# A hand-written issue order for two batches of attention and a feed-forward layer: the third batch's maxima moved

## The chip, the cores and the metric

One core of a Trainium2 chip runs the whole program. The metric is device time in microseconds (us) of one execution, the median of several runs. A core has five engines that each work through their own list of instructions in order: TensorE (PE; its weight loads are listed apart as PEld), VectorE (DVE), ScalarE (ACT), GpSimd (POOL) and SyncE (SP), which here issues all transfers. An instruction waits on semaphores for what it needs, and all that stands behind it on its engine waits with it.

## The reference

For each of 8 batches and 8 heads (576 tokens, head size 64), K and V are first condensed into 32 memories by softmax weights, then every query attends to these memories. The heads side by side are the input of a feed-forward layer (512 to 2048 to 512):

```python
a = np.exp(phi - np.max(phi, axis=2, keepdims=True))        # phi: batch, head, 576 tokens, 32 memories
a = a / (np.sum(a, axis=2, keepdims=True) + 1e-09)          # softmax over the tokens
k_m = np.einsum('bhsm,bhsd->bhmd', a, k)
v_m = np.einsum('bhsm,bhsd->bhmd', a, v)
scores = np.matmul(q, k_m.transpose(0, 1, 3, 2)) / np.sqrt(64)
attn = softmax(scores)                                      # over the 32 memories
x = np.matmul(attn, v_m)                                    # heads side by side: 4608 tokens x 512
h = x @ w_in
out = (h * np.clip(h + 3.0, 0.0, 6.0) / 6.0) @ w_out
```

All is float32 at the interface. The kernel splits operands of its matmuls into a high part (TensorE's rounded float32) and a low part, and adds three products.

## The kernel before

The product of memories V and `w_in` is taken once per batch ("fold"), so that the first layer of the feed-forward part multiplies it with the attention weights themselves. The work behind that is cut into **slots**: slot n is one tile of 128 hidden columns for one part of a batch's tokens (256 tokens, or 320, of which 64 are kept for a later slot of two batches together). Slots 0 to 71 belong to the first two batches. A slot's steps are named by a letter and its number:

- `g.n`: first matmul (L409, PE, 6 matmuls into a PSUM tile `ph`, of which there are two); `u.n`: relu (L419, ACT, into `gf`, of which there are two); `m.n`: gate (L423, DVE, reads `ph` and `gf`); `k.n`: the gate of the 64 tokens kept (L428, DVE); `h.n`, `l.n`: high and low part of the result (L437 on ACT, L441 on DVE); `a.n`: second matmul (L452, PE, 6 matmuls), which runs three slots later.

The attention part of batch b has steps of its own: `pt.b`, `pn.b` load phi transposed and in natural layout (L201), `kv.b.t` loads five tiles of K and V (L207), `q.b.half` loads queries (L213); `mx.b` takes the maxima over tokens (L236, DVE). These stand one per partition and are needed along a row: for the first two batches TensorE turns them (`md`, `me`), from the third on they go out to DRAM (`mo.b`, L241, a transfer of single values) and come back to all partitions (`sp.b`, L246, into `nmxb`). Then `xa.b.part` subtracts them (L261, DVE), `xe` is the exponential (L265, ACT), `kvm.b.t` the matmuls over tokens (L273, PE), `sc` scores (L311), `cs`, `dm`, `bl` softmax steps (L342, L354, L367, on GpSimd but for the first half of the first batch), `fo.b.c` the fold (L376, PE) and `vh`, `vl` its high and low part (L387, L392).

The weights arrive as 64-bit words and are turned into float32 by six steps on ACT and DVE (`ab`, `ro`, `cl`, `sh`, `si`, `to`); `sx.u`, `sy.u` split `w_out` (L179 on ACT, L183 on GpSimd), `wk.c` stores a finished quarter of `w_in` to DRAM (L174). `recall` (L503) reads back partial outputs, which `e0`, `e1` (L479) add to the result of a slot's last matmul, and `fetch` (L191) reads back `w_in`.

The order is written out by hand: `BEGIN` is a list of such words, and `play` issues them one by one. Each engine's list is the words that concern it, in that order:

```python
    def play(words):
        for word in words:
            name, *args = word.split(".")
            n = [int(x) for x in args]
            if name in WEIGHTS:
                WEIGHTS[name](*n)
            elif name in SLOT:
                SLOT[name](slots[n[0]])
```

From slot 72 on another table orders the batches 2 to 7; it is not touched.

Of the kernel before, what the change touches and what calls it, by code (L numbers as in the profile page):

```python
# [50 lines left out]
q.0.0 xa.0.0 xa.0.1 xe.0.0 raw2.0 xa.0.2 xe.0.1 cl.0.0.0 xe.0.2 sh.0.0.0 q.0.1 ab.0.0.1 si.0.0.0 ro.0.0.1
raw2.1 kvm.0.0 cl.0.0.1 kvm.0.1 sh.0.0.1 si.0.0.1 kvm.0.2 to.0.0.0 kvm.0.3 kvm.0.4 nr.0 to.0.0.1 nk.0 tp.0 tk.0
sc.0.0 ab.1.0 pt.1 ct.0.0 pn.1 kv.1.0 kv.1.1 kv.1.2 kv.1.3 ro.1.0 cm.0.0 kv.1.4 sc.0.1 cs.0.0 warm.4 cl.1.0
ex.0.0 ds.0.0 wk.0 ab.1.1 dr.0.0 dm.0.0 ro.1.1 q.1.0 mx.1 fo.0.0 bt.0.0 raw2.2 md.1 bh.0.0 ct.0.1 me.1 vh.0.0.0
q.1.1 warm.3 vh.0.0.1 cm.0.1 xa.1.0 raw2.3 cs.0.1 vl.0.0.0 xe.1.0 vl.0.0.1 ex.0.1 xa.1.1 kvm.1.0 sh.1.0 xe.1.1
kvm.1.1 raw.1.0 xa.1.2 si.1.0 xe.1.2 kvm.1.2 raw.1.1 kvm.1.3 raw.1.2 ds.0.1 kvm.1.4 to.1.0 raw.1.3 raw2.4
cl.1.1 sx.0 nr.1 dr.0.1 nk.1 sh.1.1 dm.0.1 bl.0.0 tp.1 raw2.5 ro.1.2 sy.0 si.1.1 tk.1 g.0 sc.1.0 u.0 g.1 bt.0.1
u.1 to.1.1 bh.0.1 ro.1.3 bl.0.1 ct.1.0 sx.1 m.0 fo.1.0 cm.1.0 h.0 ab.0.1.0 m.1 cs.1.0 g.2 l.0 g.3 h.1 sy.1
cl.0.1.0 ex.1.0 a.0 u.2 ds.1.0 vh.1.0.0 vh.1.0.1 m.2 l.1 h.2 g.4 dr.1.0 u.3 vl.1.0.0 dm.1.0 a.1 ab.0.1.1
vl.1.0.1 m.3 sc.1.1 l.2 h.3 bt.1.0 u.4 g.5 l.3 bh.1.0 ct.1.1 a.2 bl.1.0 u.5 m.4 k.4 h.4 cm.1.1 ro.0.1.0 g.6 m.5  # L60
cs.1.1 k.5 l.4 a.3 h.5 l.5 ex.1.1 sh.0.1.0 g.7 u.6 ds.1.1 e0.3 a.4 m.6 u.7 k.6 dr.1.1 h.6 m.7 g.8 dm.1.1 k.7
h.7 l.6 a.5 l.7 u.8 bt.1.1 ro.0.1.1 g.9 m.8 si.0.1.0 bh.1.1 a.6 u.9 bl.1.1 h.8 e1.3 g.10 ro.1.4 m.9 eo.3 a.7
cl.0.1.1 h.9 ro.1.5 l.8 to.0.1.0 g.11 u.10 a.8 e0.7 sh.0.1.1 ab.1.2 m.10 si.0.1.1 g.12 h.10 l.9 to.0.1.1 u.11
a.9 m.11 l.10 h.11 g.13 cl.1.2 u.12 ab.1.3 l.11 a.10 m.12 k.12 sh.1.2 u.13 g.14 e1.7 h.12 si.1.2 eo.7 fo.1.1
raw.2.0 raw.2.1 raw2.6 raw2.7 raw.2.2 raw.2.3 wk.1 m.13 a.11 k.13 h.13 l.12 to.1.2 vh.1.1.0 u.14 g.15 vh.1.1.1
raw.3.0 a.12 vl.1.1.0 sx.2 m.14 k.14 h.14 l.13 sy.2 g.16 l.14 u.15 a.13 m.15 u.16 k.15 cl.1.3 h.15 g.17
ab.0.2.0 m.16 a.14 l.15 sh.1.3 u.17 h.16 si.1.3 g.18 ro.0.2.0 a.15 m.17 k.17 h.17 l.16 to.1.3 u.18 g.19 ro.1.6
a.16 ro.0.2.1 vl.1.1.1 m.18 sx.3 l.17 g.20 cl.0.2.0 a.17 u.19 sy.3 sh.0.2.0 h.18 ro.1.7 fo.0.1 m.19 k.19 h.19
l.18 g.21 l.19 u.20 m.20 vh.0.1.0 a.18 si.0.2.0 u.21 h.20 ab.0.2.1 g.22 m.21 k.21 l.20 a.19 vl.0.1.0 u.22 h.21
to.0.2.0 vh.0.1.1 g.23 a.20 m.22 raw.3.1 raw.3.2 l.21 h.22 g.24 cl.0.2.1 u.23 a.21 ab.1.4 l.22 m.23 k.23  # L70
sh.0.2.1 u.24 g.25 h.23 si.0.2.1 ro.0.3.0 a.22 m.24 l.23 h.24 cl.1.4 g.26 u.25 e0.22 to.0.2.1 a.23 e0.23 m.25
raw.3.3 k.25 h.25 e1.22 g.27 ab.0.3.0 sh.1.4 eo.22 l.24 si.1.4 u.26 a.24 vl.0.1.1 ro.0.3.1 m.26 e1.23 g.28 h.26
l.25 eo.23 wk.2 to.1.4 u.27 a.25 fo.0.2 m.27 sx.4 k.27 l.26 g.29 cl.0.3.0 u.28 sy.4 a.26 h.27 sh.0.3.0 vh.0.2.0
vh.0.2.1 m.28 l.27 h.28 g.30 si.0.3.0 u.29 a.27 ab.0.3.1 m.29 k.29 l.28 h.29 g.31 to.0.3.0 u.30 a.28 vl.0.2.0
ab.1.5 m.30 l.29 g.32 h.30 cl.0.3.1 u.31 a.29 l.30 m.31 u.32 k.31 cl.1.5 h.31 g.33 m.32 sh.0.3.1 h.32 a.30 l.31
sh.1.5 u.33 si.0.3.1 g.34 a.31 si.1.5 m.33 k.33 h.33 l.32 g.35 to.0.3.1 u.34 a.32 to.1.5 wk.3 ab.1.6 pt.2 pn.2
kv.2.0 kv.2.1 kv.2.2 kv.2.3 kv.2.4 vl.0.2.1 sx.5 m.34 l.33 h.34 g.36 sy.5 u.35 l.34 a.33 m.35 q.2.0 u.36 k.35
cl.1.6 h.35 g.37 ab.1.7 m.36 a.34 l.35 sh.1.6 u.37 h.36 si.1.6 g.38 fo.0.3 m.37 k.37 h.37 l.36 a.35 to.1.6 u.38
vh.0.3.0 vh.0.3.1 g.39 a.36 vl.0.3.0 sx.6 m.38 l.37 h.38 sy.6 g.40 u.39 l.38 a.37 m.39 u.40 k.39 cl.1.7 h.39
# [5 lines left out]
nr.2 m.49 nk.2 k.49 h.49 tp.2 e0.46 g.50 tk.2 e1.46 sc.2.0 u.50 l.49 eo.46 a.47 m.50 ct.2.0 h.50 cm.2.0 g.51
e0.47 cs.2.0 sc.2.1 e1.47 u.51 a.48 l.50 ex.2.0 eo.47 pn.3 kv.3.0 kv.3.1 kv.3.2 kv.3.3 ct.2.1 kv.3.4 pt.3 m.51
g.52 cm.2.1 h.51 a.49 u.52 k.51 cs.2.1 l.51 m.52 fetch.2.1 g.53 ds.2.0 h.52 ex.2.1 l.52 a.50 dr.2.0 u.53 ds.2.1
q.3.0 dm.2.0 m.53 g.54 k.53 h.53 dr.2.1 recall.1.0 bt.2.0 a.51 dm.2.1 u.54 l.53 bh.2.0 recall.1.1 m.54 g.55
bl.2.0 bt.2.1 h.54 a.52 l.54 u.55 bh.2.1 m.55 k.55 h.55 g.56 bl.2.1 l.55 fo.2.0 u.56 m.56 a.53 h.56 mx.3
vh.2.0.0 vh.2.0.1 g.57 vl.2.0.0 mo.3 vl.2.0.1 a.54 u.57 l.56 m.57 k.57 h.57 g.58 l.57 a.55 u.58 m.58 h.58 g.59  # L90
l.58 a.56 u.59 m.59 k.59 h.59 g.60 sp.3 q.3.1 fetch.2.2 l.59 a.57 u.60 m.60 h.60 g.61 l.60 a.58 u.61 m.61 k.61
h.61 g.62 l.61 a.59 u.62 m.62 h.62 g.63 l.62 a.60 u.63 m.63 k.63 h.63 a.61 h.64 l.63 l.64 a.62 h.65 l.65 a.63
e0.62 h.66 e1.62 a.64 l.66 eo.62 h.67 e0.63 e1.63 h.68 a.65 l.67 l.68 h.69 a.66 eo.63 l.69 h.70 a.67 l.70 h.71
a.68 l.71
# [604 lines left out]
```

## Time and profile before

| | |
|---|---|
| median of 3 runs | 751.16 us (749.7 to 752.16) |
| the profiled execution's own time | 751.13 us |
| its span, first to last instruction | 749.4 us |
| busy: PE, DVE, ACT, POOL | 94%, 60%, 48%, 10% |

The span is what the rows below divide up; 1.7 us of the execution lie around it. Shares of busy time are means over a start in which the weights are prepared and VectorE has most to do, and a long rest in which TensorE hardly stops.

### The profile page before, as it was taken

To read this page: it belongs to the slowest core of one execution; us is meant where nothing else is said; L and a number is where in the kernel's file an instruction comes from. 1 tells how busy PE (TensorE), PEld (TensorE's weight loads), DVE (VectorE), ACT (ScalarE), POOL (GpSimd) and SP (SyncE) were. 2 spreads that over 40 slices of the span, in tenths; PEclk is the share of its full clock that TensorE was granted. 3 is DMA by queue.
4 is the path that set the end of the run, shared out by engine and by line. 5 is a ranking of instruction groups with operands and counts; after the bars stand their busy time and mean duration, and the time that the engine had idled before them with its cause. 6 is when DMAs were issued, how large, how long until landed. Compare 5 with 4: busy or idle time off the path is not lost.

```text
span 749.4 us, 12233 instructions
## 1 busy us (share of the span) xinstructions
PE 707.3 (94%) x4706; PEld 565.7 (75%) x4706; DVE 446.5 (60%) x999; ACT 361.5 (48%) x765; POOL 78.5 (10%) x59
## 2 busy tenths in 40 slices
...
GB/s 329 373 417 42 225 169 141 251 28 155 311 177 58 132 218 13 143 64 329 8 148 57 68 281 8 148 58 288 48 133 78 72 57 57 57 113 1 1 1 70
DMA packets 26042, 99.77 MB, mean 133 GB/s; under 512 B 4224, under 2 KB 4992, under 8 KB 21376
## 3 DMA queue, kind: packets, MB, share of 16 engines
...
q8 instruction: 37, 0.61, 0.4%
...
## 4 chain that ended last, share of the span: by engine, by line
PE 70%; DVE 15%; DMA 7%; ACT 3%; issue 3%; SPq 1%; ACTq 0%; DVEq 0%
PE acc L452 42%; PE ph L409 20%; PE pv L376 3%; DMA raw<-in_w 2%; DVE glo L441 2%; PE pk L273 2%; DVE gf L423 2%; DVE tmp L161 2%; DMA kvt<-in_kv 2%; DMA ptile<-in_pt 1%; DVE pnat L261 1%; PE psc L311 1%; DVE tmp L153 1%; DMA nmx<-nmx 1%; DVE tmp L156 1%
## 5 line engine op out<-in xcount | busy, mean ns | idle before, releaser
L452 PE MATMUL acc<-w,ghi 128*128 128x512 f32 x1152 | 324.7, 400 | 0.5 <-DVE o L483 0.4
L452 PEld LDWEIGHTS acc<-w,ghi 128*128 128x128 f32 x1152 | 202.3, 189 | 59.6 <-issue 16.8
L419 ACT ACTIVATE gf<-ph,three 128x256 f32<-128x256 f32 (+1 forms) x256 | 127.9, 500 | 170.9 <-PE ph L409 158.3
L409 PEld LDWEIGHTS ph<-phi,both 128*128 128x128 f32 x1024 | 164.3, 190 | 46.4 <-DVE gf L423 10.2
L423 DVE SCALAR_TENSOR_TENSOR gf<-gf,ph 128x256 f32<-128x256 f32 x256 | 106.9, 418 | 152.1 <-ACT gf L419 150.9
L409 PE MATMUL ph<-phi,both 128*128 128x320 f32 (+1 forms) x1024 | 183.2, 301 | 13.6 <-DVE rest L428 6.9
L452 PE MATMUL acc<-w,glo 128*128 128x512 f32 x576 | 184.7, 396 | 0.0
L437 ACT CAST ghi<-gf 128x256 fp32r<-128x256 f32 x256 | 103.9, 406 | 125.3 <-DVE gf L423 124.9
L441 DVE TENSOR_TENSOR glo<-gf,ghi 128x256 fp32r<-128x256 f32 x256 | 121.7, 477 | 49.4 <-ACT ghi L437 49.3
L452 PEld LDWEIGHTS acc<-w,glo 128*128 128x128 f32 x576 | 108.4, 188 | 25.6 <-DVE glo L441 0.4
L409 PE MATMUL ph<-plo,both 128*128 128x256 f32 (+1 forms) x512 | 110.2, 297 | 0.7 <-DVE plo L367 0.7
L409 PEld LDWEIGHTS ph<-plo,both 128*128 128x128 f32 x512 | 83.0, 190 | 1.0 <-DVE plo L367 1.0
L392 DVE TENSOR_TENSOR both<-pv,both 128x512 fp32r<-128x512 f32 x64 | 43.7, 688 | 42.0 <-ACT both L387 41.9
L342 POOL TENSOR_TENSOR st<-st,mx 128x640 f32<-128x640 f32 (+1 forms) x15 | 18.5, 1231 | 385.3 <-DVE mx L338 382.9
L387 ACT CAST both<-pv 128x512 fp32r<-128x512 f32 x64 | 36.6, 583 | 1.7 <-PE pv L376 1.6
L376 PE MATMUL pv<-w,kvT 64*32 64x512 f32 x512 | 35.7, 615 | 0.3 <-DVE both L392 0.3
L273 PE MATMUL pk<-kvt,pnat 128*32 128x129 f32 (+1 forms) x640 | 24.2, 295 | 9.1 <-DMA kvt<-in_kv 8.8
L273 PEld LDWEIGHTS pk<-kvt,pnat 128*32 128x32 f32 (+1 forms) x640 | 17.5, 115 | 16.5 <-ACT tmp L145 6.4
L183 POOL TENSOR_TENSOR w<-tmp,w 128x1024 fp32r<-128x1024 f32 x8 | 20.0, 2506 | 73.8 <-ACT w L179 73.8
L428 DVE SCALAR_TENSOR_TENSOR rest<-gf,ph 128x64 f32<-128x64 f32 x128 | 27.2, 213 | 0.0
L367 POOL TENSOR_TENSOR plo<-pT,phi 128x640 fp32r<-128x640 f32 (+1 forms) x15 | 21.7, 1445 | 36.6 <-ACT phi L362 36.6
L354 POOL TENSOR_TENSOR st<-st,sm 128x640 f32<-128x640 f32 (+1 forms) x15 | 17.8, 1184 | 50.2 <-DVE sm L350 50.2
...
## 6 DMA issues: line engine op xcount, KB each, us to landing
...
```

The source lines that it names most:

```text
L273: nc.tensor.matmul(self.pk[j * M : (j + 1) * M, g, :KV], self.pnat[:rows, t, g * P + j * M : g * P + (j + 1) * M], kvt[:rows, g * NJ + j, ...
L367: self.aux[hf].tensor_tensor(plo, self.pT[hf], probs[self.b, hf][0].bitcast(F32), ALU.subtract)
L376: nc.tensor.matmul(self.pv[c][j * M : (j + 1) * M, g, :], self.kvT[rows, g, j * M : (j + 1) * M], chunk[rows, j, :].bitcast(F32), start=Tr ...
L387: nc.scalar.copy(both[:, 0], self.pv[c][:, :, VC * k : VC * (k + 1)])
L392: nc.vector.tensor_tensor(both[:, 1], src, both[:, 0].bitcast(F32), ALU.subtract)
L409: nc.tensor.matmul(self.ph, w[:, g, fs], x[:, g * n : (g + 1) * n], start=(i == 0), stop=(i == len(seq) - 1),)
L419: nc.scalar.activation(self.gf, self.ph, AF.Relu, bias=three)
L423: nc.vector.scalar_tensor_tensor(gf[:, :n], gf[:, :n], 6.0, ph[:, :n], ALU.min, ALU.mult)
L428: nc.vector.scalar_tensor_tensor(kept, gf[:, n:], 6.0, ph[:, n:], ALU.min, ALU.mult)
L437: nc.scalar.copy(self.ghi, self.gated())
L441: nc.vector.tensor_tensor(self.glo, self.gated(), self.ghi.bitcast(F32), ALU.subtract)
L452: nc.tensor.matmul(accs[self.b, self.hf][0 if one else k], (self.glo if i == 2 else self.ghi)[:, k * P : (k + 1) * P], w2lo if i == 1 else ...
```

## The change

`BEGIN` is written anew. It holds the same 814 words, so every instruction and transfer is still there once; only their order differs. Two lines of the diff as an example, of slots 41 to 45:

```diff
-g.41 m.40 l.39 a.38 h.40 sh.1.7 u.41 vl.0.3.1 g.42 si.1.7 a.39 m.41 k.41 h.41 l.40 g.43 to.1.7 u.42 a.40 fo.1.2
-mx.2 sx.7 sy.7 m.42 mo.2 l.41 g.44 vh.1.2.0 vh.1.2.1 a.41 vl.1.2.0 u.43 vl.1.2.1 h.42 m.43 fo.1.3 k.43 h.43
...
+sh.1.7 sy.6 u.41 k.41 g.42 mx.2 a.39 m.41 mo.2 wk.3 vl.0.3.1 h.41 g.43 l.40 l.41 u.42 a.40 si.1.7 u.43 m.42
+fo.1.2 to.1.7 h.42 g.44 a.41 vh.1.2.0 l.42 sx.7 m.43 k.43 vl.1.2.0 g.45 h.43 sy.7 vh.1.2.1 l.43 a.42 u.44
```

`pt.2` and `pn.2` move from slot 35 to slot 27; the five `kv.2` and `q.2.0` move from slot 35 to slot 45, behind `sp.2`; `wk.3` moves from slot 35 to slot 42. `fo.2.0` moves from slot 56 to slot 62. Most other words move by less than one slot; on TensorE the order of `g` and `a` stays, and folds change places with them.

On SyncE, the transfers around the third batch's loads. Before:

```order
L174 DMA w_kept_77<-w_1042 128x2048
L174 DMA w_kept_78<-w_1280 128x2048
L201 DMA ptile<-in_pt 128x1152
L201 DMA pnat<-in_pn 128x1280
L207 DMA kvt<-in_kv 128x1032 x4
L207 DMA kvt<-in_kv 64x1032
L213 DMA qh<-in_qt 128x1024
L241 DMA nmx_1616<-nmx 128x2x1
L246 DMA nmxb<-nmx_1616 128x256
L503 DMA o<-partial_0_686 128x1024
```

And after the change:

```order
L174 DMA w_kept_77<-w_1045 128x2048
L201 DMA ptile<-in_pt 128x1152
L201 DMA pnat<-in_pn 128x1280
L241 DMA nmx_1568<-nmx 128x2x1
L174 DMA w_kept_78<-w_1277 128x2048
L246 DMA nmxb<-nmx_1568 128x256
L207 DMA kvt<-in_kv 128x1032 x4
L207 DMA kvt<-in_kv 64x1032
L213 DMA qh<-in_qt 128x1024
L503 DMA o<-partial_0_689 128x1024
```

The loads of phi no longer stand behind the store of the last quarter of `w_in`, and K, V and the first queries now stand behind the broadcast of the maxima.

On VectorE, around the third batch's maxima (`nmx<-ptile`; `tmp<-raw_7` are `si.1.7` and `to.1.7`). Before:

```order
L423 SCALAR_TENSOR_TENSOR gf<-gf,ph 128x256
L428 SCALAR_TENSOR_TENSOR rest<-gf,ph 128x64
L441 TENSOR_TENSOR glo<-gf,ghi 128x256
L171 ISA tmp<-raw_7_807,tmp 128x2048
L236 TENSOR_REDUCE nmx<-ptile 128x2
L423 SCALAR_TENSOR_TENSOR gf<-gf,ph 128x256
L441 TENSOR_TENSOR glo<-gf,ghi 128x256
```

And after the change:

```order
L428 SCALAR_TENSOR_TENSOR rest<-gf,ph 128x64
L236 TENSOR_REDUCE nmx<-ptile 128x2
L423 SCALAR_TENSOR_TENSOR gf<-gf,ph 128x256
L392 TENSOR_TENSOR both<-pv,both 128x512
L441 TENSOR_TENSOR glo<-gf,ghi 128x256 x2
L161 SCALAR_TENSOR_TENSOR tmp<-raw_7_805,tmp 128x1024
L423 SCALAR_TENSOR_TENSOR gf<-gf,ph 128x256
L171 ISA tmp<-raw_7_805,tmp 128x2048
```

The maxima now stand ahead of `m.41`, `vl.0.3.1`, `l.40`, `si.1.7` and `to.1.7`, which they followed.

On VectorE, around the first subtraction of these maxima (`pnat<-pnat,nmxb`, `xa.2.0`). Before, with `m.43` to `xa.2.1`:

```order
L423 SCALAR_TENSOR_TENSOR gf<-gf,ph 128x256
L428 SCALAR_TENSOR_TENSOR rest<-gf,ph 128x64
L441 TENSOR_TENSOR glo<-gf,ghi 128x256 x2
L423 SCALAR_TENSOR_TENSOR gf<-gf,ph 128x256
L392 TENSOR_TENSOR both<-pv,both 128x512
L261 TENSOR_TENSOR pnat<-pnat,nmxb 128x512
L423 SCALAR_TENSOR_TENSOR gf<-gf,ph 128x256
L428 SCALAR_TENSOR_TENSOR rest<-gf,ph 128x64
L392 TENSOR_TENSOR both<-pv,both 128x512
L441 TENSOR_TENSOR glo<-gf,ghi 128x256
L261 TENSOR_TENSOR pnat<-pnat,nmxb 128x512
```

And after the change, with `vl.1.2.0` to `m.46`:

```order
L392 TENSOR_TENSOR both<-pv,both 128x512
L441 TENSOR_TENSOR glo<-gf,ghi 128x256
L392 TENSOR_TENSOR both<-pv,both 128x512
L423 SCALAR_TENSOR_TENSOR gf<-gf,ph 128x256
L428 SCALAR_TENSOR_TENSOR rest<-gf,ph 128x64
L423 SCALAR_TENSOR_TENSOR gf<-gf,ph 128x256
L441 TENSOR_TENSOR glo<-gf,ghi 128x256 x2
L261 TENSOR_TENSOR pnat<-pnat,nmxb 128x512
L392 TENSOR_TENSOR both<-pv,both 128x512 x2
L261 TENSOR_TENSOR pnat<-pnat,nmxb 128x512
L423 SCALAR_TENSOR_TENSOR gf<-gf,ph 128x256
```

`m.45`, `k.45`, `l.44` and `l.45` now stand ahead of the subtraction instead of behind it, and `vl.1.3.0`, which was ahead, is behind.

## Rows read from the trace of the kernel before

**Rows 1.** The page: busy time and share of the span of each engine.

```profile
PE 707.3 (94%) x4706; PEld 565.7 (75%) x4706; DVE 446.5 (60%) x999; ACT 361.5 (48%) x765; POOL 78.5 (10%) x59
```

**Rows 2.** Five stretches: length, busy time of each engine, granted clock, DMA share, GB/s.

```profile
40.00:57.00 17.00, 10.05 (x65) 6.15 (x66) 13.71 (x18) 9.58 (x19) 9.35 (x5) 0.70 0.99 407
57.00:158.00 101.00, 95.85 (x558) 76.98 (x559) 97.23 (x183) 69.27 (x133) 18.85 (x10) 1.00 0.43 157
158.00:168.02 10.02, 9.67 (x71) 6.13 (x69) 6.51 (x11) 4.83 (x11) 2.39 (x1) 1.00 0.01 0
168.02:173.39 5.37, 0.00 (x1) 0.03 (x1) 1.30 (x4) 0.58 (x2) 0.00 (x0) 0.80 0.85 218
173.39:178.00 4.61, 4.61 (x16) 3.58 (x20) 3.70 (x10) 2.81 (x8) 0.00 (x0) 0.50 0.89 372
```

**Rows 3.** Chain that ended last, from 157 us: start, duration, what.

```profile
157.10 1.26 DVE nmx L236
158.40 7.45 DMA nmx<-nmx
165.86 6.21 DMA nmxb<-nmx
```

**Rows 4.** VectorE in order of time: start, duration, instruction, idle time before.

```profile
153.36 0.68 DVE L392 TENSOR_TENSOR both<-pv,both 128x512 fp32r<-128x512 f32 x1
155.43 0.20 DVE L428 SCALAR_TENSOR_TENSOR rest<-gf,ph 128x64 f32<-128x64 f32 x1
157.03 1.34 DVE L236 TENSOR_REDUCE nmx<-ptile 128x2 f32<-128x1152 f32 x1
158.62 2.31 DVE L441 TENSOR_TENSOR glo<-gf,ghi 128x256 fp32r<-128x256 f32 x1
...
172.09 0.69 DVE L261 TENSOR_TENSOR pnat<-pnat,nmxb 128x512 f32<-128x512 f32 x1 [7.27 <-DMA nmxb<-nmx]
172.70 0.41 DVE L423 SCALAR_TENSOR_TENSOR gf<-gf,ph 128x256 f32<-128x256 f32 x1
```

**Rows 5.** TensorE in order of time, slots 43 and 47, with `a.40` and `a.44`.

```profile
156.21 0.76 PE L409 MATMUL ph<-phi,both 128*128 128x320 f32 x4
158.03 0.63 PE L452 MATMUL acc<-w,glo 128*128 128x512 f32 x2
...
173.39 1.41 PE L409 MATMUL ph<-phi,both 128*128 128x320 f32 x4 [5.37 <-DVE rest L428]
176.83 1.05 PE L452 MATMUL acc<-w,glo 128*128 128x512 f32 x2
```

**Rows 6.** SyncE's issues in order of time (rows of several cover the waits between).

```profile
117.60 18.92 SPq L174 DMA_DIRECT2D w_kept<-w  x2
138.00 3.66 SPq L207 DMA_DIRECT2D kvt<-in_kv  x5
165.86 0.33 SPq L246 DMA_DIRECT2D nmxb<-nmx  x1
```

**Rows 7.** Issue to landing: of `mo` and `sp` together, of K and V.

```profile
DMA to landing us min/median/max: 5.7/7.5/9.4
...
DMA to landing us min/median/max: 5.6/9.4/13.0
```

**Rows 8.** The start, 40 to 57 us: GpSimd, VectorE and TensorE in order of time.

```profile
42.23 2.79 POOL L183 TENSOR_TENSOR w<-tmp,w 128x1024 fp32r<-128x1024 f32 x1
...
41.07 1.75 DVE L367 TENSOR_TENSOR plo<-pT,phi 128x512 fp32r<-128x512 f32 x1
42.74 3.37 DVE L161 SCALAR_TENSOR_TENSOR tmp<-raw,tmp 128x1024 uint32<-128x1024 uint32 x1
52.53 0.60 DVE L441 TENSOR_TENSOR glo<-gf,ghi 128x256 fp32r<-128x256 f32 x1 [2.48 <-ACT ghi L437]
53.74 2.18 DVE L153 TENSOR_SCALAR tmp<-tmp 128x1024 f32<-128x1024 f32 x1 [0.61 <-ACT tmp L145]
...
56.89 0.86 PE L409 MATMUL ph<-phi,both 128*128 128x320 f32 x4 [2.50 <-DVE gf L423]
```

**Rows 9.** GpSimd and VectorE at `sy.7` and `si.1.7`, in order of time.

```profile
158.26 2.39 POOL L183 TENSOR_TENSOR w<-tmp,w 128x1024 fp32r<-128x1024 f32 x1 [7.44 <-ACT w L179]
...
153.96 1.21 DVE L161 SCALAR_TENSOR_TENSOR tmp<-raw,tmp 128x1024 uint32<-128x1024 uint32 x1
155.56 0.41 DVE L441 TENSOR_TENSOR glo<-gf,ghi 128x256 fp32r<-128x256 f32 x1
```

More of the change, by code (lines that the diff above doesn't have):

```diff
@@ L50 @@
 pt.0 raw.0.0 raw.0.1 pn.0 raw.0.2 raw.0.3 kv.0.0 kv.0.1 kv.0.2 mx.0 kv.0.3 md.0 me.0 kv.0.4 ab.0.0.0 ro.0.0.0
[L51 to L79, printed above, removed]
```

55 lines of the change are left out of this document (42 added, 13 removed).

## The prediction, as it was put on record

> **What bounds the kernel now.** I read the page's busy shares first: TensorE works 94% of the span, VectorE 60% [rows 1], so TensorE's idle time is what can be won. The table of stretches shows where it lies [rows 2]. From 57 to 158 us TensorE is busy 95.85 of 101.00 us and VectorE 97.23: both are nearly full there, and neither has more than a few us to give. Then, from 168.02 to 173.39 us, TensorE does nothing at all for 5.37 us, and in the 4.61 us after it works at a granted clock of 0.50, the 1.2 GHz level. Behind that the kernel stays bound by TensorE.
>
> The chain of waits says what the hole is made of [rows 3]: the third batch's maxima end, `mo.2` takes 7.45 us out to DRAM and `sp.2` 6.21 us back, and only then can `xa.2.0` run. VectorE waits 7.27 us in front of it [rows 4], with `m.45` behind it at 172.70. TensorE's `g.47` needs the PSUM tile that `m.45` and `k.45` free, hence its 5.37 us, and the row names L428 as what ended them [rows 5].
>
> What this costs: `g.43` and `a.40` take 156.21 to 158.66, 2.45 us, at the full clock; the same pair one hole later, `g.47` and `a.44`, takes 173.39 to 177.88, 4.49 us, at the low one [rows 5]. So the hole costs 5.37 + 2.04 = 7.4 us.
>
> **The change, part by part.**
>
> *The maxima earlier.* Their load `pt.2` stands behind `wk.3` before, in a pair of stores that takes until 136.52 [rows 6]; now it is issued after `wk.2` alone, so its data are there long before. What counts is the place of `mx.2` on VectorE, which was not waiting for data at 157.03 but for its turn. Five instructions step behind it, `vl.0.3.1` to `to.1.7`; they began at 153.36 and reached to 157.03, 3.67 us, of which `k.41`'s 0.13 (155.43 to the next at 155.56) stays ahead [rows 4, 9]. So `mx.2` ends about 3.5 us earlier, at 154.9 instead of 158.37. Its two transfers are not shortened: 154.9 + 7.45 + 6.21, with about 0.05 of issue, gives 168.6 us for `xa.2.0`. From one side, all landings of these two kinds lie between 5.7 and 9.4 us [rows 7]; a first leg of 9.4 would make it 170.6. I take the pair's own durations, as the queue is as empty then (0 GB/s from 158 on [rows 2]) but for `wk.3`, which is now issued behind `mo.2` and not ahead of it.
>
> *More work in front of the wait.* VectorE's list up to `xa.2.0` now holds `m.45`, `k.45`, `l.44` and `l.45`. That lets TensorE go on with `g.47` and `a.44` where it stopped before: from 168.0 it has another 2.45 us, to 170.5. The next, `g.48`, needs `m.46`, which follows `xa.2.0` (0.61 to the next start [rows 4]), two `vl` of about 0.67, `xa.2.1` and itself: some 3.0 us. So 168.6 + 3.0 = 171.6, and TensorE's hole shrinks from 5.37 to about 1.1 us; with the slow first leg to 3.1. The clock: a hole of 2.50 us ahead of 56.89 [rows 8] was followed by a stretch at 1.00 [rows 2], one of 5.37 us by 0.50. A hole of 1.1 us is nearer the first, so I charge nothing for the clock. Gain: 7.4 - 1.1 = 6.3 us, bounds 7.4 (no hole) and 2.3 (3.1 us of hole, and the 2.04 of the clock after all).
>
> *K, V and queries later.* They were on chip from 138 us on with time to spare [rows 6]; now they are issued when `mo.2` has landed, 154.9 + 7.5 = 162.4, behind `sp.2`. A tile of 516 KB at the 372 GB/s of the stretch after 173.39 [rows 2] takes 1.4 us. If they land in line behind `sp.2` at 168.6, the first is there at 170.0 and the fifth, half as large, at 174.9; `kvm.2.0` stands behind `g.48`, about 172.6, and the others follow at one or two per slot of 2.45 us, so the last is wanted after 180. `q.2.0` and the first `recall` follow at 176.3 and 177.7; `e0.46` wants that one behind `a.46`, near 179. I take nothing for it. The other bound: the slowest landing of K and V is 13.0 us from issue [rows 7], so 162.8 + 13.0 = 175.8 for the first tile, and `kvm.2.0` would hold TensorE's list for 3.2 us.
>
> *`wk.3`, `fo.2.0` and the rest behind.* Nothing reads the last quarter of `w_in` back for many slots; `fo.2.0` at slot 62 is covered by slots 64 to 71, whose second matmuls alone hold TensorE for eight times the 1.56 us of such a step (157.10 to 158.66). SyncE's order from `q.2.0` on is the old one. Nothing for these; without that cover two `vl` of 0.68 [rows 4] would lie bare, 1.4 us.
>
> *The start.* VectorE's work ahead of each slot changes by less than a slot's worth, so what can differ is how often it is held. Between 41 and 57 us it idles 2.48 and 0.61 us, and three instructions are held while GpSimd works: `bl.0.0` takes 1.75 (the like-sized `xa.2.0` 0.69), `si.1.1` 3.37 (`si.1.7` 1.21), `cl.0.1.0` 2.18 (`vl.0.3.1`, as wide, 0.68) [rows 8, 4, 9]: together 1.06 + 2.16 + 1.50 + 3.09 = 7.8 us. Now `bl.0.0` goes ahead of the reciprocal that releases `dm.0.1`, `h.0` stands two steps closer to the front on ScalarE, and `cl.0.1.0` comes behind slot 5's gate; but the GpSimd work is the same, and `to.1.1`, `l.0` and `l.1` now meet it. Following the rows through, I expect about 6 us of holds in place of 7.8: a gain of 1.5 us after rounding down. Bounds: a gain of 5 (TensorE has 5.15 us of idle time from 57 to 158 [rows 2], and VectorE, as full, has less) and a loss of 3 (all holds stay and `l.1` adds one as long as `sy.7`'s 2.39 [rows 9]).
>
> **Sum**: 751.13 - 6.3 - 1.5 = 743.3 us. The profiled execution is within 0.03 us of the runs' median, so that stands for the median too.
>
> **The holds by GpSimd: row and rule.** `l.41` takes 2.31 us and ends with `sy.7`, which began 0.36 us before it; `l.40` took 0.41 [rows 4, 9]. So an instruction that meets such work pays up to its length. The Trainium skill, page "GPSIMD Engine Reference", section "8. Key points", says that GpSimd shares its SBUF interfaces with VectorE and contends with VectorE instructions in a two-port mode or with two SBUF inputs; `glo<-gf,ghi` has two, and the trace agrees. By that rule an order is worth as much as the instructions that it lets meet GpSimd's, which speaks against a plain transfer of the rows above to the new order; it is the third rival.
>
> **The rivals.**
>
> 1. *The stall moves to K and V or the recall.* For it: ten transfers now stand behind `sp.2` on SyncE, and six of them were issued 20 us earlier before [rows 6]. Against it: bandwidth, as worked out. Price: 3.2 us, so 743.3 + 3.2 = 746.5, with the low clock after it 748.5.
> 2. *The wait at `xa.2.0` stays.* The load moves by eight slots, the maxima by only 3.5 us, and both legs stay 13.7 us. If VectorE reaches `xa.2.0` as much earlier, or TensorE can't use `m.45`, the hole is 5.4 - 3.5 = 1.9 us and the clock's 2.04 are paid again: a gain of 7.4 - 3.9 = 3.5, and 747.6 us; with a first leg of 9.4 us 749.6, no change.
> 3. *Slower: GpSimd holds VectorE longer from 57 to 158 us.* Ten GpSimd instructions lie there, 18.85 us together, beside a VectorE that is busy 97.23 of 101 us [rows 2], so each hold goes to the end of the stretch. It decides when the new order adds more than 6.3 + 1.5 + 2.3 = 10.1 us to what is held there now; at that it is 753.4, at the most 751.13 - 7.8 + 18.85 = 762.2, and I would put it at 755. Against it: in the rows such holds exist already, so much of the 18.85 is paid.
>
> **How the numbers follow.** Differences within 0.3%, 2.25 us, I call no change, about what a measurement of this kernel can tell. The forecast, 739 to 746.5, gets 0.62. The first rival gets 0.13, nearly all faster (0.11, and 0.02 no change). The second gets 0.13, divided at 748.9 (0.07 and 0.06). The third gets 0.12 (0.08 slower, 0.04 no change). Faster 0.80, no change 0.12, slower 0.08. The range reaches from the forecast's best start with no hole, 751.13 - 7.4 - 5 = 738.7, a us lower for rounding, to the second rival's 749.6: 737.7 to 750.
>
> **What would show it.** In the profile after: `xa.2.0` ready about 13.7 us after `mx.2` ends; TensorE's largest hole between slots 42 and 52 at most 3 us; no stretch at 0.50 between slots 10 and 71; `kvm.2.0` to `kvm.2.4` not released by a transfer; `e0.46` not by the recall. The start is right if `g.4`, at 56.89 us before [rows 8], starts 2 to 4 us earlier and half of that is still there at slot 42. The prediction fails if K and V land later than 4 us behind `sp.2`, if the first leg grows beside `wk.3`, or if TensorE loses more than 7 us between slots 4 and 42.

## The result and the profile after

The changed kernel takes 742.41 us in the median (742.34 to 743.0), the kernel before 750.99 us in the same set (749.7 to 752.16): a ratio of 0.9888, interval 0.9871 to 0.9905. A second set gave 742.51 us (741.2 to 743.97) and 0.9885, 0.9865 to 0.9905. The forecast was 743.3 us, with a range of 737.7 to 750. The profiled execution took 742.35 us; its span is 740.6 us against 749.4.

The page's busy shares of the changed kernel, against [rows 1]:

```profile
PE 703.9 (95%) x4706; PEld 563.6 (76%) x4706; DVE 444.6 (60%) x999; ACT 360.7 (49%) x765; POOL 81.8 (11%) x59
```

Its table of stretches, cut as [rows 2] are: the start, 57 to 158 us, up to TensorE's hole, the hole, and the work behind it.

```profile
40.00:57.00 17.00, 11.44 (x92) 7.46 (x92) 15.40 (x26) 11.38 (x21) 11.52 (x6) 0.90 0.99 408
57.00:158.00 101.00, 96.27 (x570) 77.65 (x563) 96.74 (x183) 70.10 (x136) 20.49 (x10) 1.00 0.41 124
158.00:166.41 8.41, 7.84 (x52) 5.54 (x50) 5.39 (x9) 3.43 (x9) 1.72 (x1) 1.00 0.54 162
166.41:168.13 1.72, 0.00 (x1) 0.00 (x0) 1.72 (x5) 0.97 (x3) 0.00 (x0) 1.00 1.02 377
168.13:178.00 9.87, 9.87 (x114) 7.17 (x115) 3.77 (x11) 3.48 (x9) 0.00 (x0) 1.00 1.04 324
```

The hole is 1.72 us in place of 5.37, and the clock column stays at 1.00 behind it, where [rows 2] have 0.50. In the start the column has 0.90 in place of 0.70. VectorE in the changed kernel, in order of time (start, duration, instruction, idle time before): `mx.2`, `l.43`, `xa.2.0`, then `e0.46` with `e1.46`.

```profile
149.53 1.34 DVE L236 TENSOR_REDUCE nmx<-ptile 128x2 f32<-128x1152 f32 x1
...
157.59 2.41 DVE L441 TENSOR_TENSOR glo<-gf,ghi 128x256 fp32r<-128x256 f32 x1 [0.56 <-ACT ghi L437]
...
165.26 0.69 DVE L261 TENSOR_TENSOR pnat<-pnat,nmxb 128x512 f32<-128x512 f32 x1 [2.49 <-DMA nmxb<-nmx]
...
177.56 1.29 DVE L479 SCALAR_TENSOR_TENSOR o<-acc,o 128x512 f32<-128x512 f32 x2 [2.63 <-DMA o<-partial]
```

VectorE waits 2.49 us for the broadcast where it waited 7.27 [rows 4], and has a new wait of 2.63 us for the first `recall`. SyncE's issues of `mo.2`, `sp.2` and `kv.2`, and then, from the chain that ended last, that `recall` (issue, time until it landed):

```profile
150.90 0.38 SPq L241 DMA_DIRECT2D nmx<-nmx  x1
...
159.08 0.32 SPq L246 DMA_DIRECT2D nmxb<-nmx  x1
159.44 4.85 SPq L207 DMA_DIRECT2D kvt<-in_kv  x5
```

```profile
164.97 12.51 DMA o<-partial
```

TensorE in the changed kernel: the start of `g.4`, the last matmuls of `a.31` and `a.40`, `g.48` behind the hole, `tp.2` behind the new wait, the last matmuls of `a.60`.

```profile
52.92 0.75 PE L409 MATMUL ph<-phi,both 128*128 128x320 f32 x4
...
132.92 0.63 PE L452 MATMUL acc<-w,glo 128*128 128x512 f32 x2
...
153.95 0.64 PE L452 MATMUL acc<-w,glo 128*128 128x512 f32 x2
...
168.13 0.74 PE L409 MATMUL ph<-phi,both 128*128 128x256 f32 x4 [1.72 <-DVE gf L423]
...
179.88 0.44 PE L295 MATMUL pq<-ident,kvn 128*128 128x128 f32 x2 [1.09 <-ACT kvn L290]
...
211.23 0.63 PE L452 MATMUL acc<-w,glo 128*128 128x512 f32 x2
```

The same matmuls of `a.31` and `a.60` in the kernel before:

```profile
133.81 0.64 PE L452 MATMUL acc<-w,glo 128*128 128x512 f32 x2
...
219.99 0.64 PE L452 MATMUL acc<-w,glo 128*128 128x512 f32 x2
```

Since `g` and `a` keep their order on TensorE, the ends of the same step can be compared in every kernel. That divides the time into legs: each column has the time from the end of the step before to the end of the step that it names. The first leg starts with `g.0`, whose own start differs by some 1.6 us between executions. All in us, each from one profiled execution:

| kernel | `g.0` starts | to `a.24` | to `a.31` | to `a.40` | to `a.43` | to `a.60` | rest | median |
|---|---|---|---|---|---|---|---|---|
| before | 41.26 | 74.46 | 18.73 | 24.21 | 9.36 | 52.60 | 528.8 | 750.99 |
| changed | 41.68 | 73.65 | 18.22 | 21.04 | 9.54 | 47.73 | 528.7 | 742.41 |
| changed, again | 41.29 | 73.22 | 18.23 | 21.03 | 9.55 | 47.39 | 528.7 | 742.51 |
| old up to 35 | 42.21 | 73.34 | 18.72 | 22.47 | 9.55 | 48.29 | 528.7 | 745.15 |
| new up to 34 | 41.55 | 74.49 | 18.22 | 24.36 | 9.36 | 52.52 | 528.6 | 749.66 |
| old up to 24 | 42.47 | 73.19 | 19.72 | 21.10 | 9.61 | 47.93 | 529.7 | 744.84 |
| maxima alone | 41.25 | 73.35 | 18.75 | 25.10 | 9.36 | 47.16 | 528.6 | 745.42 |
| slots 32 to 41 alone | 42.19 | 73.10 | 18.75 | 21.84 | 9.68 | 51.04 | 528.7 | 749.24 |
| `ro.1.2` back | 41.53 | 75.89 | 18.23 | 21.04 | 9.55 | 47.07 | 528.7 | 745.68 |
| `sx` earlier | 40.84 | 73.93 | 18.19 | 22.94 | 9.54 | 49.26 | 528.7 | 745.61 |
| `kv` early | 41.95 | 74.42 | 18.22 | 21.04 | 9.54 | 46.43 | 528.7 | 742.08 |
| `m.46` up | 41.43 | 73.25 | 18.23 | 21.03 | 9.58 | 44.62 | 528.7 | 738.90 |
| `cl.1.3` back | 42.40 | 71.62 | 18.41 | 21.04 | 9.58 | 44.44 | 528.7 | 737.53 |

Of the 8.8 us between the two spans, 0.4 lie ahead of the end of `a.24`, 0.5 in slots 25 to 31, 3.2 in slots 32 to 40, and 4.9 from `a.43` to `a.60`; 0.2 are lost between `a.40` and `a.43`. From `a.24` to `a.43` the legs repeat to less than 0.1 us where the orders are the same. The first leg does not: six traces of the new start scatter from 73.22 to 74.49, five of the old from 73.10 to 74.46.

### The profile page after: what moved, and what is told of

Read it like the earlier page. It is cut to its first block, busy times and chain, and to the rows that moved or that the text cites. A ratio compares the mean times of both kernels' runs of the same rounds, so it can differ in the third digit from the quotient of the medians.

```text
span 740.6 us, 12236 instructions
## 1 busy us (share of the span) xinstructions
PE 703.9 (95%) x4706; PEld 563.6 (76%) x4706; DVE 444.6 (60%) x999; ACT 360.7 (49%) x765; POOL 81.8 (11%) x59
## 4 chain that ended last, share of the span: by engine, by line
PE 79%; DVE 7%; DMA 7%; ACT 3%; issue 2%; SPq 0%; POOL 0%; ACTq 0%; DVEq 0%; POOLq 0%
PE acc L452 48%; PE ph L409 24%; PE pv L376 4%; DMA raw<-in_w 3%; DMA kvt<-in_kv 3%; PE pk L273 2%; DMA o<-partial 2%; DVE glo L441 1%; PE psc L311 1%; DVE gf L423 1%; DVE pnat L261 1%; ACT gf L419 1%; DVE tmp L161 1%; DVE o L483 1%; DVE tmp L153 1%
## 5 line engine op out<-in xcount | busy, mean ns | idle before, releaser
L183 POOL TENSOR_TENSOR w<-tmp,w 128x1024 fp32r<-128x1024 f32 x8 | 21.9, 2739 | 73.4 <-ACT w L179 56.9
```

## The experiments

All of them change `BEGIN` alone, so every kernel holds the same words; the pieces shown are pieces of that list, with the changed kernel as the base unless another is named. Ratios are to the kernel before. The table above has each under a short name.

**Which half gives what.** In the first kernel the list is the old one up to `to.1.5` (slot 35) and the new one behind it; in the second the new one up to `to.0.3.1` (slot 34) and the old one behind.

```diff
-raw2.4 nk.1 bl.0.0 sx.0 tp.1 dr.0.1 g.0 si.1.1 tk.1 dm.0.1 sc.1.0 u.0 raw2.5 ro.1.2 g.1
+dr.0.1 nk.1 sh.1.1 dm.0.1 bl.0.0 tp.1 raw2.5 ro.1.2 sy.0 si.1.1 tk.1 g.0 sc.1.0 u.0 g.1
...
 l.32 g.35 to.0.3.1 u.34 a.32 to.1.5
 pt.2 pn.2 vl.0.2.1 ab.1.6 l.33 fo.0.3 m.34 u.35 h.34 g.36
```

> Old issue order up to slot 35, new order from there (with the third batch's load, maximum and broadcast in their early place). Theory 'two separate gains' (start 3.9 us, hole 5.9 us, less 1.1 us lost to the wait for the recall): only the hole's gain is left, so about 751.0 - (8.8 - 3.9) = 746.1 us, g.4 at 56.9, no stretch of low clock between a.44 and g.48. Rival 'the start gives nothing that lasts, since the third batch's broadcast is late by the start's gain': within 0.5 us of the changed kernel, 742.4.

745.15 us (743.16 to 747.3), ratio 0.9926, interval 0.9904 to 0.9947: near the first theory's 746.1. The granted clock did fall, but behind `g.48`: it was 0.79 from 170 to 178 us.

```diff
 a.31 m.33 k.33 h.33 l.32 to.0.3.1
-g.35 u.34 a.32 vl.0.2.1 ab.1.6 l.33 fo.0.3 m.34 u.35 si.1.5
+si.1.5 g.35 u.34 a.32 to.1.5 wk.3 ab.1.6 kv.2.0 kv.2.1 kv.2.2
```

> New issue order up to slot 34, old order from there, so that the third batch's maximum stands in its old place. Theory 'two separate gains': the start's 3.9 us alone, about 751.0 - 3.9 = 747.1 us, g.4 at 52.9 and a hole of TensorE with a low clock behind a.43 as in the kernel before. Rival 'the early start is eaten again by the hole, which ends with the broadcast': 750 to 751.

749.66 us (748.76 to 751.52), ratio 0.9987, interval 0.9975 to 0.9999. Neither reading holds: the start's gain is gone, but not in the hole. TensorE in this kernel, `g.4` and the last matmuls of `a.40`:

```profile
53.02 0.75 PE L408 MATMUL ph<-phi,both 128*128 128x320 f32 x4
...
157.99 0.63 PE L451 MATMUL acc<-w,glo 128*128 128x512 f32 x2
```

`g.4` starts 3.87 us earlier than before, and `a.40` ends at 158.62, where it ended before (158.66) [rows 5]. What the new start wins is spent on the way, and the 4 us by which the changed kernel is ahead at `a.40` are won elsewhere. So the theory of two gains gave way to another: the start ends up worth nothing, and slots 32 to 40 give what it seemed to give (theory H in the runs below).

**The step that waits for a transfer.** `ro.1.2` on ScalarE wants a piece of the weights that lands at about 45 us. In the old list `tk.1`, which TensorE waits for, stood behind it.

```diff
-g.0 si.1.1 tk.1 dm.0.1 sc.1.0 u.0 raw2.5 ro.1.2 g.1
+g.0 si.1.1 ro.1.2 tk.1 dm.0.1 sc.1.0 u.0 raw2.5 g.1
```

> The changed kernel with the one step ro.1.2 moved back ahead of tk.1, where it stood before. Theory A (the start's gain came from ScalarE, which no longer waits some 3.9 us for that step's transfer ahead of the transposes): 1.5 to 4 us slower, 744 to 746, with sc.1.0 late again. Theory B (the gain came from shorter holds of VectorE by GpSimd): 742.4 within 0.3.

746.84 us, ratio 0.9941, interval 0.9921 to 0.9961: 4.4 us slower than the changed kernel, a little more than theory A's 1.5 to 4. One of the six executions, the profiled one, took 3853.57 us, and its trace tells nothing of the edit, which was run once more.

> The changed kernel with the one step ro.1.2 back ahead of tk.1, for its trace (the run of this edit before had 746.8 us in the median and an odd profiled execution). Theory H (the start's 4 us are spent again by slot 17; what is left at slot 40 comes from the holds of VectorE behind sy.5 and sy.6): g.4 late at about 56.5, and yet a.31 within 1 us of the changed kernel's 133.55, so that the 4.4 us must show behind slot 31, as holds that came back. Theory S (the start's gain is carried to the end): a.31 and a.40 both about 4 us late, at 137.5 and 158.5.

745.68 us (743.81 to 747.04), ratio 0.992, interval 0.9889 to 0.9952; the profiled execution took 743.81. ScalarE in this kernel, and then TensorE's `sc.1.0`:

```profile
44.24 1.16 ACT L149 ACTIVATE raw<-raw 128x1024 uint32<-128x1024 uint32 x1 [2.02 <-DMA raw<-in_w]
45.29 0.35 ACT L299 COPY kvT<-pq 128x256 f32<-128x256 f32 x1
```

```profile
45.70 1.11 PE L311 MATMUL psc<-qh,kvT 64*32 64x256 f32 x16 [3.20 <-ACT kvT L299]
```

In the changed kernel `tk.1` (the copy into `kvT`) runs at 42.27 us and the same wait is harmless behind it:

```profile
42.27 0.38 ACT L299 COPY kvT<-pq 128x256 f32<-128x256 f32 x1
...
45.31 1.14 ACT L149 ACTIVATE raw<-raw 128x1024 uint32<-128x1024 uint32 x1 [2.16 <-DMA raw<-in_w]
```

The place of this step is worth 1.4 to 2.7 us at the end of `a.24` (75.89 against the 73.22 to 74.49 of the other traces of the new start), and from there every leg is as in the changed kernel. The medians of the two sets lie 4.4 and 3.3 us above 742.41; why that is more than in this trace, of the fastest execution of its set, is open. Both theories of the second run miss: `a.31` ended at 135.65, 2.1 us behind the changed kernel, and no hold came back behind it. What this step wins is carried to the end, then; but without it the new start is slower than each of the five old ones, so the rest of the new start gives away what the step wins.

**Where the start's gain goes back.** The old list up to the end of `a.24`, the new one behind it (the base shown is the kernel before):

```diff
 sh.1.4 eo.22 l.24 si.1.4 u.26 a.24
-vl.0.1.1 ro.0.3.1 m.26 e1.23 g.28 h.26 l.25 eo.23 wk.2
+e1.23 eo.23 wk.2 pt.2 pn.2 vl.0.1.1 m.26 l.25 h.26 g.28
```

> The order before up to slot 24, the changed kernel's order from there (the third batch early). Theory H (the new start is spent by slot 24, and the gain ahead of the hole comes from slots 25 to 40): 742.4 within 1 us, with g.4 late at about 56.5 and 39.3 us from the end of a.24 to that of a.40. Theory S (the start's gain is carried): some 3.9 us slower than the changed kernel, 746.3.

744.84 us (743.63 to 745.94), ratio 0.9914, interval 0.9895 to 0.9933: between the two. The old start reaches `a.24` in 73.19 us from `g.0`, as fast as the new one, and `a.31` to `a.40` take 21.10: that much is theory H's. The 1.5 us in slots 25 to 31 (19.72 against 18.23) come from the seam, where `si.1.4` and `e1.23` now stand ahead of `m.26` together and `g.28` waits 1.49 us. The rest of its distance, `g.0`'s own start and 0.9 us behind `a.60` at a granted clock of 0.95, is open.

**The maxima alone, and the slots alone.** Both start from the kernel before. First the third batch's load, maxima and broadcast:

```diff
 h.26 l.25 eo.23 wk.2
+pt.2 pn.2
 to.1.4 u.27 a.25
...
 a.38 h.40 sh.1.7 u.41
+mx.2 mo.2
 vl.0.3.1 g.42 si.1.7
```

> The kernel before with the third batch alone moved: pt.2 and pn.2 behind wk.2, mx.2 and mo.2 ahead of vl.0.3.1; all else, xa.2.0's place too, as before. The maxima end some 3.5 us earlier, so xa.2.0 starts near 168.6 and g.47 near 169.9, a hole of 1.9 us in place of 5.4. Theory (the hole hangs on mx.2's end): 3.5 us gained and, if the clock no longer falls, 2.0 more: 745.5 to 747.5. Rival (the broadcast alone does nothing, since m.45 still stands behind it): 750 to 751.

745.42 us (744.65 to 747.92), ratio 0.9923, interval 0.9898 to 0.9948. Its stretches: the hole, and the work behind it.

```profile
167.81:169.15 1.34, 0.01 (x2) 0.03 (x1) 1.30 (x4) 0.58 (x2) 0.00 (x0) 1.00 1.06 436
169.15:178.00 8.85, 8.85 (x111) 6.62 (x111) 4.55 (x12) 4.12 (x11) 0.00 (x0) 1.00 0.47 195
```

`xa.2.0` started at 167.85 us, `g.47` at 169.15, and the clock stayed up. The leg from `a.43` to `a.60` took 47.16 us in place of 52.60. So the move that the title names gives 5.4 us there by itself; `mx.2`, 1.34 us long, now lies in front of it and lengthens that leg by 0.9 us (25.10 against 24.21). Then only the steps of slots 32 to 41:

```diff
 l.31 sh.1.5 u.33 si.0.3.1 g.34 a.31
-si.1.5 m.33 k.33 h.33 l.32 g.35 to.0.3.1 u.34 a.32 to.1.5
+m.33 k.33 h.33 l.32 to.0.3.1 g.35 u.34 a.32
...
 a.38 h.40 sh.1.7 sy.6 u.41 vl.0.3.1 g.42 si.1.7 a.39
```

> The kernel before with only the steps of slots 32 to 41 in the changed kernel's order; the start, the load, the maximum and the broadcast keep their old places. Theory H: l.34 and l.38 no longer meet sy.5 and sy.6 (2.0 us each), a.40 ends 2 to 4 us earlier, mx.2 with it, and the whole program: 747 to 749. Rival (the gain at slot 40 needs the new start): 750 to 751.

749.24 us (747.04 to 751.9), ratio 0.9969, interval 0.995 to 0.9987. `a.31` to `a.40` took 21.84 us in place of 24.21, 2.4 us with the old start, as theory H said. The median is 1.7 us lower, the interval of the ratio reaches from 1.0 to 3.8 us, and the profiled execution took 747.14. In its trace `l.34` and `l.38` take 0.42 and 0.41 us; `si.1.7` meets `sy.6` instead and takes 2.82. TensorE's hole stays at 5.20 us, with the maxima in their old place. The leg with the hole is 1.6 us shorter even so, with a granted clock of 0.79 from 170 to 178 us where the kernel before had 0.58.

**The hold itself.** Why slots 32 to 40 are faster is seen where GpSimd and VectorE meet. GpSimd in the kernel before, `sy.5` and `sy.6`:

```profile
138.46 2.39 POOL L183 TENSOR_TENSOR w<-tmp,w 128x1024 fp32r<-128x1024 f32 x1 [16.19 <-ACT w L179]
148.19 2.63 POOL L183 TENSOR_TENSOR w<-tmp,w 128x1024 fp32r<-128x1024 f32 x1 [7.34 <-ACT w L179]
```

VectorE at those times, `l.34`, and `l.37` with `l.38` in one row:

```profile
138.73 2.41 DVE L441 TENSOR_TENSOR glo<-gf,ghi 128x256 fp32r<-128x256 f32 x1 [0.15 <-ACT ghi L437]
...
148.14 2.97 DVE L441 TENSOR_TENSOR glo<-gf,ghi 128x256 fp32r<-128x256 f32 x2
```

`l.34` ends at 141.14, as `sy.5` does but for 0.29 us, and takes 2.41 us for what takes 0.42 elsewhere; `l.38` the same. In the changed kernel:

```profile
139.61 2.80 POOL L183 TENSOR_TENSOR w<-tmp,w 128x1024 fp32r<-128x1024 f32 x1 [16.50 <-DVE glo L441]
148.36 2.81 POOL L183 TENSOR_TENSOR w<-tmp,w 128x1024 fp32r<-128x1024 f32 x1 [5.96 <-ACT w L179]
```

```profile
138.19 0.42 DVE L441 TENSOR_TENSOR glo<-gf,ghi 128x256 fp32r<-128x256 f32 x1
...
140.77 0.41 DVE L423 SCALAR_TENSOR_TENSOR gf<-gf,ph 128x256 f32<-128x256 f32 x1
141.10 1.59 DVE L441 TENSOR_TENSOR glo<-gf,ghi 128x256 fp32r<-128x256 f32 x1
```

`l.34` is through before `sy.5` starts; beside it run mostly gates, which read PSUM and keep their usual time, until `l.36` meets its end and pays 1.17. Beside `sy.6` stands `mx.2`, which takes its usual 1.34 us. To test it, the changed kernel with the two GpSimd steps and what they wait for on ScalarE a little earlier:

```diff
-to.1.5 a.33 vh.0.3.0 vh.0.3.1 m.35 k.35 h.35 l.34 g.37 sx.5 cl.1.6 l.35 a.34 u.36 sh.1.6 sy.5
+to.1.5 a.33 sx.5 sy.5 vh.0.3.0 vh.0.3.1 m.35 k.35 h.35 l.34 g.37 cl.1.6 l.35 a.34 u.36 sh.1.6
...
-to.1.6 g.40 a.37 u.40 m.39 k.39 h.39 cl.1.7 g.41 sx.6 m.40 l.39 a.38 h.40 sh.1.7 sy.6
+to.1.6 g.40 a.37 sx.6 sy.6 u.40 m.39 k.39 h.39 cl.1.7 g.41 m.40 l.39 a.38 h.40 sh.1.7
```

> The changed kernel with sx.5 and sx.6 (ScalarE) and sy.5 and sy.6 (GpSimd) each a few places earlier, so that the two GpSimd instructions start about 0.5 to 0.7 us earlier and meet l.35 and l.39 on VectorE. Same work, same start. Theory H: two holds of about 2.0 and 1.8 us come back and the one of 1.2 at l.36 goes, so a.40 is 2.6 to 3.8 us later and mx.2 with it: 745 to 746. Rival (VectorE has room for a hold there): 742.4 within 0.5.

745.61 us (743.13 to 746.27), ratio 0.9915, interval 0.9887 to 0.9943. VectorE in this kernel, `l.35` and `l.39`:

```profile
139.64 1.55 DVE L441 TENSOR_TENSOR glo<-gf,ghi 128x256 fp32r<-128x256 f32 x1 [0.99 <-ACT ghi L437]
...
148.72 2.03 DVE L441 TENSOR_TENSOR glo<-gf,ghi 128x256 fp32r<-128x256 f32 x1
```

The holds came back where they were expected, a little smaller (1.1 and 1.6 us), with a wait of 0.99 us ahead of the first. `a.31` to `a.40` took 22.94 us in place of 21.04. The hole behind grew to 3.14 us, with a granted clock of 0.79 from 170 to 178 us: the maxima end 0.7 us later against `a.43` (152.90 and 165.44), and from their end to `xa.2.0` it was 15.1 us in place of 14.4 (14.8 in the second trace of the changed kernel). That makes 3.1 us in the median for four words moved. The theory stands, with 1.9 us in place of 2.6 to 3.8 for the slots. The other 1.3 of the 3.2 us that the changed kernel gains there are not shown by this run.

**The new wait for the recall.** The changed kernel with the third batch's `kv.2` and `q.2.0` back at slot 35:

```diff
 m.33 k.33 h.33 l.32 to.0.3.1
+kv.2.0 kv.2.1 kv.2.2 kv.2.3 kv.2.4 q.2.0
 g.35 u.34
...
-u.45 m.45 sp.2 kv.2.0 kv.2.1 fo.1.3 kv.2.2 kv.2.3 kv.2.4 k.45 q.2.0 recall.0.0
+u.45 m.45 sp.2 fo.1.3 k.45 recall.0.0
```

> The changed kernel with the third batch's kv loads and its first q load moved back to their early place on SP's queue (slot 35), so that the recall's load is issued behind the broadcast without them. Theory: the wait of 2.63 us for the recall's transfer goes, with its gap of 1.09 us on TensorE, 742.4 - 1.1 = 741.3. Rival (the gap is hidden or another wait takes its place): 742.4 within 0.3.

742.08 us (741.51 to 743.15), ratio 0.9883, interval 0.9861 to 0.9905. In the trace the wait and its gap are gone, and the leg from `a.43` to `a.60` is 1.3 us shorter (46.43 against 47.73). The medians differ by 0.3 us, which is inside their scatter and nearer to the rival's 742.4 than to the theory's 741.3; only the trace speaks for the theory. This trace's first leg was 0.8 us longer, with the same words. In the second trace of the changed kernel the gap ahead of `tp.2` was 0.33 us, so the wait costs 0.3 to 1.1.

**A better order.** The changed kernel once more for a base, and on top of the edit just shown `vl.1.3.0`, `vl.1.3.1`, `m.46`, `h.46` and `l.46` ahead of the wait for the broadcast:

> The changed kernel once more, unedited, beside the three others of this set: 742.4 us, and a second trace of it, which shows how much of the differences at slots 4 to 24 is the scatter of one execution.

742.51 us.

```diff
-vh.1.3.0 recall.0.1 xa.2.0 vh.1.3.1 vl.1.3.0 u.46 g.47 vl.1.3.1 xe.2.0 q.2.1 xa.2.1 a.44 u.47 m.46
+vh.1.3.0 recall.0.1 vh.1.3.1 vl.1.3.0 u.46 vl.1.3.1 m.46 h.46 l.46 xa.2.0 g.47 xe.2.0 q.2.1 xa.2.1 a.44 u.47
```

> The changed kernel with kv.2 and q.2.0 back at slot 35 and, new, m.46 with l.46, vl.1.3.0 and vl.1.3.1 put ahead of xa.2.0 on VectorE, so that g.48 no longer waits for the broadcast. Theory (what is left of the hole is m.46's place behind xa.2.0): the gap of 1.72 us ahead of g.48 goes, and with the recall's 1.1: 742.4 - 1.1 - 1.7 = 739.6. Rival (the hole moves to g.49 or g.50, which want m.47 and m.48 behind the broadcast): 741.3 to 742.4.

738.9 us (738.43 to 740.71), ratio 0.9843, interval 0.9818 to 0.9869. TensorE in this kernel: `a.44`, and `g.48` right behind it.

```profile
165.17 0.62 PE L452 MATMUL acc<-w,glo 128*128 128x512 f32 x2
165.63 0.64 PE L409 MATMUL ph<-phi,both 128*128 128x256 f32 x4
```

No gap over 0.25 us is left between `a.43` and `a.60`, and that leg is 44.62 us. The broadcast still takes as long; VectorE has work in front of it that lasts until it lands. Last, on top of that, `cl.1.3` moved behind `m.16`:

```diff
-g.16 l.14 sy.2 u.15 cl.1.3 a.13 u.16 vh.1.1.1 m.15 k.15 h.15 m.16 g.17 sh.1.3
+g.16 l.14 sy.2 u.15 a.13 u.16 vh.1.1.1 m.15 k.15 h.15 m.16 cl.1.3 g.17 sh.1.3
```

> The kernel with m.46 up, and cl.1.3 moved behind m.16 on VectorE, so that m.15, k.15 and m.16 no longer stand behind the 2.88 us for which cl.1.3 is held by sy.2, and TensorE's gap of 1.78 us ahead of g.17 can go. Theory C (VectorE's order sets that gap and the gain is carried): 1.0 to 1.8 us below the kernel with m.46 up alone. Rival (it is spent again by slot 40, as the start's was, since VectorE's work is the same): equal to it within 0.4 us.

737.53 us (737.1 to 738.45), ratio 0.9819, interval 0.9801 to 0.9838. VectorE around `sy.2`, `cl.1.3` and what follows it, in the kernel with `m.46` up:

```profile
85.53 2.88 DVE L153 TENSOR_SCALAR tmp<-tmp 128x1024 f32<-128x1024 f32 x1
88.33 0.41 DVE L423 SCALAR_TENSOR_TENSOR gf<-gf,ph 128x256 f32<-128x256 f32 x1
88.66 0.21 DVE L428 SCALAR_TENSOR_TENSOR rest<-gf,ph 128x64 f32<-128x64 f32 x1
```

And with `cl.1.3` back, `m.15` to `cl.1.3`:

```profile
86.77 0.42 DVE L423 SCALAR_TENSOR_TENSOR gf<-gf,ph 128x256 f32<-128x256 f32 x1 [0.26 <-ACT gf L419]
87.11 0.21 DVE L428 SCALAR_TENSOR_TENSOR rest<-gf,ph 128x64 f32<-128x64 f32 x1
87.33 0.42 DVE L423 SCALAR_TENSOR_TENSOR gf<-gf,ph 128x256 f32<-128x256 f32 x1
87.67 1.66 DVE L153 TENSOR_SCALAR tmp<-tmp 128x1024 f32<-128x1024 f32 x1
```

TensorE's gap of 1.78 us ahead of `g.17` is gone, `a.24` is reached in 71.62 us from `g.0`, 1.6 us sooner, and the next legs lose 0.2 of it. So a gain in slot 17 does reach the end, as theory C had it, and this one hold accounts for some 1.6 us of the changed kernel's first leg; in the old list `sy.2` costs TensorE 0.56 us ahead of `g.17`.

## Why the prediction was right, and where only its sum was

**The maxima.** `mx.2` ends at 150.87, 3.72 us before `a.40` does, and it was 0.29 us before [rows 4, 5]: 3.4 us earlier against TensorE, where the forecast had 3.5. The maxima alone gave a leg 5.4 us shorter, so the mechanism is shown. The two transfers took 8.2 and 6.1 us, the first 0.7 more than forecast and within its bound of 9.4 [rows 7]; `xa.2.0` starts 14.4 us behind the end of `mx.2`, not 13.7. That is not the store `wk.3` behind it: with the maxima alone moved, where `wk.3` had long been issued, the first leg took 8.0 us.

**The hole.** TensorE did go on with `g.47` and `a.44`, and `g.48` followed `xa.2.0` by 2.87 us (forecast 3.0). The hole is 1.72 us in place of the 1.1 foreseen, for the most part by the longer first leg (2.11 in the second trace), and the clock stayed at 1.00. By the forecast's own count that is 7.4 - 1.7 = 5.7 us where it had 6.3. What the added work in front gives by itself is not shown. With the maxima alone, the hole was 1.34 us and the leg as short, but there they end 14.22 us ahead of `a.43`, and in the changed kernel 13.26.

**K, V and the recall.** Nothing was taken for these, and here the forecast missed. The first `recall` landed at 177.48; that this is near the 177.7 worked out is chance, for the broadcast ahead of it landed at 165.2 and not at 168.6. From there to the recall it was 12.3 us where the forecast has 9.1, and `e0.46` wanted it after 9.8, nearly the 10.4 foreseen. So the time of the transfers behind `sp.2` was mis-sized, by 3.2 us; why they took longer is open. The wait cost TensorE 1.09 us, the first rival in small. `kvm.2.0` to `kvm.2.4` were not held, although the fifth tile came some 10 us behind the broadcast. The sign set for this, 4 us, was too strict: by the forecast's own sum that tile comes 6.3 us behind. Hole and recall together make -4.6 us; a gap of 0.60 us ahead of `g.59`, which the changed kernel lacks, makes it -5.2; the leg shows -4.9, and the 0.3 between them are open.

**The start.** The term was 1.5 us, with the test that `g.4` be 2 to 4 us earlier and half of it be there at slot 42. `g.4` was 3.97 us earlier and `a.43` 3.89, so the test passed, and it proves the wrong thing. VectorE between 41 and 57 us in the changed kernel, `to.1.1`, `l.0` and `l.1`:

```profile
43.39 2.17 DVE L171 CUSTOM_DVE_ANT_0 tmp<-raw,tmp 128x2048 uint16<-128x2048 uint16 x1
...
48.70 1.57 DVE L441 TENSOR_TENSOR glo<-gf,ghi 128x256 fp32r<-128x256 f32 x1 [0.88 <-ACT ghi L437]
...
51.28 2.54 DVE L441 TENSOR_TENSOR glo<-gf,ghi 128x256 fp32r<-128x256 f32 x1
```

Against the 1.18, 0.42 and 0.41 us that these take alone they are held for 4.3 us, and with 0.88 and 0.35 us of idle time that is 5.5 by the forecast's count, near its 6. (Its 0.68 for `cl.0.1.0` alone was read off an instruction half as wide; others of its kind take 0.68 too.) What failed is that this would last. The term was too small by 2.4 us, and its place was wrong: holds decide it in part, as the forecast said, but those of slots 32 to 40 (a leg 3.2 us shorter, 1.9 of it shown to be holds), not the three between 41 and 57 us. The forecast's list of what is held [rows 8] left out `l.34` and `l.38`, whose neighbour `l.41` it quoted [rows 4, 9].

Of what moved `g.4` a good part was no hold but `ro.1.2`, which no longer stands ahead of `tk.1`: from the start of `g.0` to that of `g.4` it is 11.24 us in the changed kernel, 13.41 with that step back, and 14.0 to 15.6 in the five old starts. How much of the rest is the granted clock from 40 to 57 us (0.59 to 0.70 in the five old starts, 0.70 to 0.90 in the new ones) no run separates.

The start's gain is given back by the end of `a.24`. From 57 us to there VectorE has five held instructions in either kernel: they take 1.25, 1.26, 1.14, 2.60 and 1.84 us before, and 1.49, 1.49, 2.05, 2.88 and 2.45 changed. Less what the like take alone (0.41; 0.68 for the third of both and the fourth changed), that is 5.8 us of holds before and 7.8 after. The fourth is `cl.1.3`, with TensorE's gap of 1.78 us, where the old list has `l.13` and 0.56.

So 743.3 came out 0.9 us from the measured time by two misses that cancel: 2.4 us too little ahead of the hole, 1.4 too much behind it. That it came so near is luck. Against the third rival: GpSimd did hold VectorE at other places, and between 57 us and the end of `a.24` for 2.0 us more, but far from the 10.1 us more that the rival needs, and in slots 32 to 40 for 2.8 us less.

The Trainium skill, page "GPSIMD Engine Reference", section "8. Key points", says that GpSimd contends with VectorE instructions in a two-port mode or with two SBUF inputs. These traces agree: `glo<-gf,ghi` has two such inputs and takes up to 2.54 us in place of 0.42, the gates that read PSUM keep their 0.41. That `cl.1.3`, with one input, takes 2.88 us in place of 0.68 fits the rule only if it runs in such a mode, which no run here shows; that 0.68 us is little beside the 1.21 of `si.1.7`, as wide and with two inputs [rows 9], is no more than a hint.
